# One branch for all left-over work, row numbers at the seam, spread planning, and global keys filled once, in a fused attention and mixture-of-experts kernel

## The chip, the cores and the metric

The kernel runs on one core of a Trainium2 chip. The metric is the time of one execution on the device in microseconds (us), where less is better. A core has a matrix engine (PE, with its weight loads listed as PEld), a vector engine (DVE), a scalar engine (ACT), a general engine (POOL), and SP, which here only issues DMAs. Each takes its own list of instructions in order and waits for the others by semaphores. An indirect DMA (gather or scatter by row numbers) is issued by POOL.

## The reference

An attention over 4 batches, 8 heads, 768 positions and 64 features feeds a mixture of experts with one expert for each token.

```python
scores = q @ k.T / sqrt(64)                       # per batch and head
keep   = (key < 8) | (0 <= query - key < 96)      # 8 global keys, 96 local ones
scores = where(keep, scores - slope[head] * dist, -1e9)
x      = softmax(scores) @ v                      # -> 3072 tokens of 512 features

logits = x @ w_gate + modality_bias[modality_id]  # 8 experts
e      = argmax(logits);  g = softmax(logits)[e]
out    = g * (relu(x @ w1[e]) @ w2[e])            # 512 -> 1024 -> 512
```

## The kernel before

**Attention.** The 3072 queries are 24 blocks of 128, six for each batch (`NB`). `step(n)`, for n from 0 to 24, writes down by hand the order of PE, ACT and DVE. It works on several blocks at once: scores of block n (`s_mm`, L257), maximum and bias (`red`, DVE L276) and exponential (ACT L287) of its eight heads; transposes of the probabilities of block n-1 (`t_mm` L301, `t_cp` L310 on DVE or L308 on ACT); probabilities times V of block n-2 (`pv`, L322 with the local V rows `vl`, L334 with `vo` and `va`), its scaling (`xr`, L355) and its store; the gate logits of older blocks (`gate_a`, `gate_b`, `gate_c`); and the transposes of the next block's keys and queries (`k_mm` L215, `k_cp`: keys by ACT L228, queries by DVE L224). The lists of POOL and SP are made by a scheduler, which also decides where anything stands that the hand-written order leaves open.

**Keys.** The key store `kt` has fourteen slots of 72 columns, two for each block and two ahead of them. A slot begins with the 8 global keys. These come with the batch's first block, and POOL copies them into the other slots: L231 two for each block, L233 one for a batch. The scores read whole slots.

**Routing.** `at(n, f)` adds f to the end of step n. Each batch's tokens are routed in parts (`route_a`, `route_b`, `route_d`), and `route_c` has POOL scatter the token numbers into a sorted list in memory (`ids_sorted`, L450). When two batches are routed, `plan_e` works out on DVE, in four parts, the first three expert slots (e0 to e2). For these, `ld_x` asks for the token lists (`uie`, L618), `gather_x` gathers the tokens (L623), `ld_w` loads weights, and `split` splits these into a high part (ACT, L656) and a low part (DVE, L657). `copyv` is POOL's copy of V rows into `vo` (L135, L137).

**Experts.** `x_t` transposes the gathered tokens (L668) and splits them (ACT L671, DVE L672); `l1_unit` is the first layer (L685 to L687, results L691 and L692), `l2` the second (L723 to L725). `fin` multiplies by the gate and has POOL scatter the result (L738) by row numbers `oi`, made at L730 from the token list. Fourteen slots follow one another in a hand-written order.

**The end.** Tokens that fit into no slot are left to a loop, and other values of `n_global` and `n_local` to a general path. With these inputs neither has work:

```python
    general = nc.values_load(flag[0:1, 0:1], min_val=0, max_val=1)
    with tc.If(general):
        general_path()
    ...
    count = nc.values_load(lcnt[0:1, 0:1], min_val=0, max_val=NLT)
    with tc.For_i(0, count, 1) as g:
```

Of the kernel before, what the change touches and what calls it, by code (L numbers as in the profile page):

```python
# [9 lines left out]
F32 = mybir.dt.float32  # L10
# [9 lines left out]
P = 128  # L20
# [47 lines left out]
def moe_attention_kernel(ctx, tc, q, k, v, n_global, n_local, modality, w_gate, mod_bias, w1, w2, out):  # L68
# [141 lines left out]
    def k_mm(n, which):  # L210

        bank = p_t(f"tr{n}_{which}")
        src = kqn[n][which]
        for hp in range(NP):
            nc.tensor.transpose(  # L215
                bank[:, hp * P : (hp + 1) * P], src[:, 2 * hp : 2 * hp + 2].rearrange("p h d -> p (h d)"), ident
            )
        kqn[n][which] = bank

    def k_cp(n, which):  # L220
        bank, i = kqn[n][which], n % NB
        if which:
            qts[n] = pp.tile([P, NP, P], F32, tag="qt", name=f"qt{n}", bufs=2)
            V.tensor_copy(qts[n].rearrange("p a b -> p (a b)"), bank)  # L224
            return
        slot = kt[:, :, PER * (i + 1) : PER * (i + 2)].rearrange("p a (c w) -> p a c w", w=CH)
        view = bank.rearrange("p (a c w) -> p a c w", a=NP, c=2)
        last[0] = nc.scalar.copy(slot[:, :, :, NG0:], view)  # L228
        first = kt[:, :, PER + NG0 : PER + 2 * NG0]
        for c in range(2):  # L230
            nc.gpsimd.tensor_copy(slot[:, :, c, 0:NG0], first)  # L231
        if i == 0:
            nc.gpsimd.tensor_copy(kt[:, :, CH : CH + NG0], first)  # L233
# [325 lines left out]
    def granules(uex, ust, uli):  # L559
# [38 lines left out]
        V.tensor_copy(lcnt, m)  # L598
        yield
# [30 lines left out]
    def ld_w(s, parts="ab"):  # L630
        if "a" in parts:
            s.e = nc.sync.value_load(s.e_src, min_val=0, max_val=E - 1)
        e = s.e
        for which, src in (("a", w1), ("b", w2)):
            if which not in parts:
                continue
            for c in range(4):
# [89 lines left out]
    def fin(s, ts, parts=1):  # L727
        if 0 in ts:
            s.oi = idp.tile([P, 2], I32, tag="oi", name=f"oi{s.name}")
            V.tensor_tensor(s.oi[:, 0 : s.halves], s.ui[:, 0 : s.halves, 0], s.inv, ALU.add)  # L730
        for t in ts:
            ob = mp.tile([P, DM], F32, tag="ob", name=f"ob{s.name}{t}", bufs=2)
            gate = s.ui.bitcast(F32)[:, t, 1:2]
            n = DM // parts
            nc.scalar.mul(ob[:, 0:n], s.po[t][:, 0:n], gate)  # L735
            if parts == 2:
                V.tensor_scalar(ob[:, n:], s.po[t][:, n:], gate, None, ALU.mult)
# [200 lines left out]
    flag = const.tile([P, 1], I32, name="flag")  # L938
    lte = const.tile([P, NLT], I32, name="lte")
# [128 lines left out]
    for j in range(4):  # L1068
        at(LAST + j // 2, plan_e)
# [12 lines left out]
    at(LAST + 1, lambda: ld_w(eslots[0], "a"))  # L1082
    at(LAST + 3, lambda: [ld_x(s) for s in eslots])
    at(LAST + 4, lambda: [gather_x(s) for s in eslots[:GE]])
    for j in range(4):
        at(LAST + (4, 5, 6, 6)[j], split, None, "a", j)
    at(LAST + 4, lambda: ld_w(eslots[0], "b"))

    def l1_first(f):
        if f == 0:  # L1090
            x_t(eslots[0], 0)
            x_t(eslots[0], 1)
            l1_begin(eslots[0])
        l1_unit(eslots[0], f)
# [22 lines left out]
    def step(n):  # L1117
# [25 lines left out]
        if more:  # L1143
# [105 lines left out]
    for u in range(nslot):  # L1249
# [28 lines left out]
        else:  # L1278
            fin(s, [s.halves - 1], 2)
# [12 lines left out]
    wrawb = None  # L1292
    wraw = ctx.enter_context(tc.tile_pool(name="wraw2", bufs=8))
    wsp = wspb = ctx.enter_context(tc.tile_pool(name="wsp2", bufs=1))
    xgp = ctx.enter_context(tc.tile_pool(name="xgp2", bufs=1))
    idp = ctx.enter_context(tc.tile_pool(name="idp2", bufs=1))
    mp = ctx.enter_context(tc.tile_pool(name="mp2", bufs=1))
    count = nc.values_load(lcnt[0:1, 0:1], min_val=0, max_val=NLT)
    with tc.For_i(0, count, 1) as g:
        iv = idp.tile([P, 1], F32, tag="iv", name="iv")  # L1300
        V.tensor_copy(iv, ltv[:, ds(g, 1)])
        s = mk("l", lte[0:1, ds(g, 1)], lto[0:1, ds(g, 1)], iv, xd, 1)
        s.straight = False
        ld_x(s)
        ld_w(s)
        gather_x(s)
        x_t(s, 0)
        for c in range(4):
            split(s, "a", c)
        l1_begin(s)  # L1310
        for fh in range(2):
            l1_gran(s, fh)
            split(s, "b", 2 * fh)
            split(s, "b", 2 * fh + 1)
            l1_gran_t(s, fh)
        for c in range(8):
            l2(s, c, 0)
        fin(s, [0])
# [38 lines left out]
```

## Time and profile before

| | |
|---|---|
| median of 3 runs | 521.53 us (519.7 to 525.9) |
| the profiled execution | 518.35 us |
| its span in the trace | 516.2 us |
| mean granted PE clock | 0.961 |
| first scores of step 0 / 1 / 2 | 13.34 / 19.35 / 26.75 us |
| a usual step | 6.46 us (step 4 at 40.60, step 5 at 47.06) |
| steps 19 to 22 begin | 141.41, 149.45, 157.21, 172.55 us |
| last output scatter issued | 502.74 us |

The time includes some 2 us around the span. Times inside the trace are counted from the span's start. A row of the timeline gives the start, the duration, the engine, the line, the operation with its output and input, and in brackets the idle time before it and what ended that. A suffix q (SPq, POOLq) is the engine's sequencer: loads of registers, branches, DMA issues.

### The profile page before, as it was taken

Reading aid. Unit: us, or ns where it says so; the run is one execution under the profiler, and the core shown is the slowest. Engines: PE = TensorE matmul, PEld = TensorE weight load, DVE = VectorE, ACT = ScalarE, POOL = GpSimd, SP = SyncE. Lnnn points to the kernel's source line nnn. Section 1 sums busy time; section 2 is a strip of 40 time slices with the busy share of each in tenths; the row PEclk is TensorE's granted clock in tenths of the full one; section 3 lists DMA queues with packets and bytes.
Section 4 is the critical chain, followed back from the end, with each engine's and each line's share of the span. In section 5 each row is a group of like instructions: output and inputs, shape, how many; then the busy total and the mean of one; then the engine's idle time right before and its main releaser. Section 6 shows DMA issues by size and latency. Waiting matters only on the chain.

```text
span 516.2 us, 15203 instructions
## 1 busy us (share of the span) xinstructions
PE 472.8 (92%) x5789; PEld 423.2 (82%) x5789; DVE 340.9 (66%) x992; ACT 297.3 (58%) x716; POOL 162.3 (31%) x282
## 2 busy tenths in 40 slices
PE   4889999999985988999999999899999999999980
PEld 4778899899874867898989898798978998798960
DVE  2488788888893883788874657564765658557410
ACT  3668777777754672555454557554665558545420
POOL 9703414545552354042322215204041031400110
PEclk8599999999999898999999999999999999999995
DMA  9678889778676736367877658778597667953100
GB/s 179 143 211 189 193 190 210 178 169 209 142 203 184 235 125 187 130 247 236 251 236 234 236 197 295 248 248 273 163 332 254 227 228 250 332 187 123 42 23 23
DMA packets 125508, 102.74 MB, mean 199 GB/s; under 512 B 96283, under 2 KB 97715, under 8 KB 125428
## 3 DMA queue, kind: packets, MB, share of 16 engines
q1 hardware_dynamic: 120660, 88.65, 59.6%
q0 software_dynamic: 4768, 13.05, 7.1%
q8 instruction: 47, 0.77, 0.6%
q14 instruction: 33, 0.27, 0.2%
HBM read 87.31 MB, written 14.63 MB: 197 GB/s over the span
## 4 chain that ended last, share of the span: by engine, by line
PE 77%; DVE 7%; ACT 5%; DMA 3%; issue 3%; SPq 2%; POOL 0%; POOLq 0%; ACTq 0%; DVEq 0%
PE s L257 6%; PE phs L687 6%; PE phs L685 6%; PE phs L686 6%; PE pt L301 5%; PE pos L725 5%; PE pos L724 5%; PE pos L723 5%; PE x L334 4%; PE tr L215 3%; ACT pr L287 3%; PE x L322 3%; PE phe L685 2%; PE phe L686 2%; PE phe L687 2%
## 5 line engine op out<-in xcount | busy, mean ns | idle before, releaser
L287 ACT ACTIVATE pr<-sc,nmx 128x168 f32<-128x168 f32 x192 | 81.1, 423 | 42.0 <-DVE nmx L276 42.0
L687 PE MATMUL phs<-xhs,als 128*128 128x256 f32 x256 | 72.5, 283 | 0.5 <-DVE als L657 0.5
L685 PE MATMUL phs<-xhs,ahs 128*128 128x256 f32 x256 | 72.2, 282 | 0.0
L686 PE MATMUL phs<-xls,ahs 128*128 128x256 f32 x256 | 72.1, 282 | 0.0
L623 POOL DMA_INDIRECT xgs<-x_rows,uis x16 | 27.5, 1716 | 130.5 <-DMA uis<-ids_sorted 66.6
L276 DVE CUSTOM_DVE_ANT_0 sc<-s,tbl 128x168 f32<-128x168 f32 x192 | 52.2, 327 | 21.4 <-PE s L257 18.2
L301 PE MATMUL pt<-ident,pr 128*128 128x128 f32 x288 | 47.7, 290 | 9.7 <-DVE pT L310 6.7
L692 DVE SCALAR_TENSOR_TENSOR hls<-phs,hhs 128x512 fp32r<-128x512 f32 x32 | 22.1, 692 | 50.4 <-ACT hhs L691 50.4
L257 PEld LDWEIGHTS s<-kt,qt 64*64 64x64 f32 x1536 | 40.6, 139 | 15.9 <-POOL kt L233 7.7
L257 PE MATMUL s<-kt,qt 64*64 64x128 f32 (+1 forms) x1536 | 44.6, 258 | 9.5 <-POOL kt L233 6.7
L723 PE MATMUL pos<-bhs,hhs 128*128 128x512 f32 x128 | 51.4, 401 | 0.0
L725 PE MATMUL pos<-bhs,hls 128*128 128x512 f32 x128 | 50.6, 395 | 0.0
L724 PE MATMUL pos<-bls,hhs 128*128 128x512 f32 x128 | 50.5, 395 | 0.0
L687 PEld LDWEIGHTS phs<-xhs,als 128*128 128x128 f32 x256 | 48.8, 191 | 0.8 <-DVE als L657 0.7
L685 PEld LDWEIGHTS phs<-xhs,ahs 128*128 128x128 f32 x256 | 48.9, 191 | 0.4
L686 PEld LDWEIGHTS phs<-xls,ahs 128*128 128x128 f32 x256 | 48.8, 191 | 0.4
L691 ACT ACTIVATE hhs<-phs 128x512 fp32r<-128x512 f32 x32 | 19.1, 597 | 49.8 <-PE phs L687 49.8
L310 DVE COPY pT<-pt 128x384 f32<-128x384 f32 x71 | 39.1, 550 | 9.6 <-PE pt L301 9.4
L301 PEld LDWEIGHTS pt<-ident,pr 128*128 128x128 f32 x288 | 32.4, 145 | 15.5 <-DVE pT L310 8.0
L450 POOL DMA_INDIRECT ids_sorted<-tki,pi x24 | 24.6, 1023 | 39.6 <-DVE remb L508 23.6
L287 ACT ACTIVATION_READ_ACCUMULATOR pr<-sc,nmx 128x1 f32 x192 | 35.9, 187 | 0.0
L738 POOL DMA_INDIRECT out<-obs,ois x16 | 17.1, 1069 | 47.6 <-ACT obs L735 39.7
(340 smaller groups left out, 1257.6 us busy)
## 6 DMA issues: line engine op xcount, KB each, us to landing
va<-in_v SPq DMA_DIRECT2D x25, 256.0 KB, 3.5
kn<-in_k SPq DMA_DIRECT2D x24, 256.0 KB, 4.9
qn<-in_q SPq DMA_DIRECT2D x24, 256.0 KB, 4.8
x_rows<-xr SPq DMA_DIRECT2D x24, 256.0 KB
vl<-in_v SPq DMA_DIRECT2D x84, 32.0 KB, 3.3
rawe0a<-in_moe_w SPq DMA_DIRECT2D x4, 512.0 KB, 3.6
rawe0b<-in_moe_w SPq DMA_DIRECT2D x4, 512.0 KB, 3.6
rawe1a<-in_moe_w SPq DMA_DIRECT2D x4, 512.0 KB
```

The lines of the kernel that those rows point to most:

```text
L257: nc.tensor.matmul(ps[h][64 * half : 64 * half + 64, c : c + cnt], qt[hs, hp, 64 * half : 64 * half + 64], keys, start=True, stop=True,)
L276: V.tensor_tensor_reduce(out=sc, in0=pss[n, hp // 2][h][:, hp % 2 * W : (hp % 2 + 1) * W], in1=(tbl0 if n % NB == 0 else tbl)[:, hh, :], o ...
L287: last[0] = nc.scalar.activation(pr[:, h * (PRW - W) : h * (PRW - W) + W], sc, AF.Exp, bias=nmx[:, hh : hh + 1], scale=-1.0, accum_out=sum ...
L301: nc.tensor.transpose(tp[:, j * P : (j + 1) * P], pr[:, o : o + P], ident)
L310: V.tensor_copy(pT.rearrange("p a b -> p (a b)"), tp[:, 0 : 3 * P])
L623: nc.gpsimd.indirect_dma_start(out=s.xg[:, t, :], out_offset=None, in_=s.xsrc, in_offset=bass.IndirectOffsetOnAxis(ap=s.ui[:, t, 0:1], axi ...
L685: nc.tensor.matmul(o, hi[:, fs], s.xh[:, c, :], start=(c == 0), stop=False)
L686: nc.tensor.matmul(o, hi[:, fs], s.xl[:, c, :], start=False, stop=False)
L687: nc.tensor.matmul(o, lo[:, fs], s.xh[:, c, :], start=False, stop=(c == 3))
L723: nc.tensor.matmul(s.po[t], s.hh[:, fc, tt], hi[:, wv], start=(fc == 0), stop=False)
L724: nc.tensor.matmul(s.po[t], s.hh[:, fc, tt], lo[:, wv], start=False, stop=False)
L725: nc.tensor.matmul(s.po[t], s.hl[:, fc, tt], hi[:, wv], start=False, stop=(fc == 7))
```

## The change

1. **One branch.** A flag `past`, which is the larger of "tokens left over" and the general path's flag, is worked out with the plan. A single `If` on it encloses the general path and the left-over loop.
2. **Row numbers.** `rows_out` makes `oi` for e0 to e2 after the last gate instead of where the scheduler had put it.
3. **Plan.** The four parts of `plan_e` stand in steps 17, 18, 18, 19 (18, 18, 19, 19 before).
4. **Splits.** The four weight splits of e0 stand in steps 21, 22, 23, 24 (22, 23, 24, 24 before), and its first weights are loaded in two pieces, in steps 19 and 20.
5. **Global keys.** With a batch's first block all slots are filled at once: DVE fills slots 1 to 3, POOL slots 4 to 13.
6. **Queries and keys of block 1** (positions 128 to 255) are transposed in step 0 behind its scores, and copied behind four of its heads.
7. **Seam.** The token transposes of e0 stand ahead of block 23's `pv`, its first layer behind that, and the last gates are reordered.
8. **Last output.** Both halves on ACT (before, one on ACT and one on DVE).
9. Constants are loaded and made a step later, the zeroing of the list (`consts_c`) one piece for each step.

```diff
-        bank = p_t(f"tr{n}_{which}")
+        bank = (p_p if n == 1 else p_t)(f"tr{n}_{which}")
...
-        first = kt[:, :, PER + NG0 : PER + 2 * NG0]
-        for c in range(2):
-            nc.gpsimd.tensor_copy(slot[:, :, c, 0:NG0], first)
         if i == 0:
-            nc.gpsimd.tensor_copy(kt[:, :, CH : CH + NG0], first)
+            first = kt[:, :, PER + NG0 : PER + 2 * NG0].unsqueeze(2)
+            for eng, c0, c1 in ((V, 1, 4), (nc.gpsimd, 4, 2 * NB + 2)):
+                eng.tensor_copy(slots[:, :, c0:c1, 0:NG0], first.broadcast_to([P, NP, c1 - c0, NG0]))
...
+        V.tensor_scalar(m, m, 1.0, None, ALU.min)
+        V.tensor_copy(m2, flag)
+        V.tensor_tensor(m, m, m2, ALU.max)
+        V.tensor_copy(past, m)
...
+    def rows_out(s):
+        s.oi = idp.tile([P, 2], I32, tag="oi", name=f"oi{s.name}")
+        V.tensor_tensor(s.oi[:, 0 : s.halves], s.ui[:, 0 : s.halves, 0], s.inv, ALU.add)
...
-            n = DM // parts
-            nc.scalar.mul(ob[:, 0:n], s.po[t][:, 0:n], gate)
-            if parts == 2:
-                V.tensor_scalar(ob[:, n:], s.po[t][:, n:], gate, None, ALU.mult)
+            nc.scalar.mul(ob, s.po[t], gate)
...
-    at(0, consts_l)
-    at(2, consts_b)
+    at(1, consts_l)
+    at(3, consts_b)
     for j in range(8):
-        at(3 + j // 2, consts_c, j)
-    at(3, consts_d)
+        at(3 + j, consts_c, j)
+    at(4, consts_d)
...
-        at(LAST + j // 2, plan_e)
+        at(LAST - 1 + (0, 1, 1, 2)[j], plan_e)
...
-    at(LAST + 1, lambda: ld_w(eslots[0], "a"))
+    at(LAST + 1, lambda: ld_w(eslots[0], "a", (0, 1)))
+    at(LAST + 2, lambda: ld_w(eslots[0], "a", (2, 3)))
...
-        at(LAST + (4, 5, 6, 6)[j], split, None, "a", j)
+        at(LAST + (3, 4, 5, 6)[j], split, None, "a", j)
...
             s_mm(n, 1)
+            if not n:
+                k_mm(1, 0)
+                k_mm(1, 1)
             for hh in (0, 2, 1, 3, 4, 6, 5):
                 red(n, hh)
+                if not n and hh == 3:
+                    k_cp(1, 0)
+                    k_cp(1, 1)
...
-    l1_first(0)
+    x_t(eslots[0], 0)
+    x_t(eslots[0], 1)
+    l1_begin(eslots[0])
     rinv(NBLK - 1)
     pv(NBLK - 1)
+    gate_a(*gates(NBLK - 2))
     gate_c(*gates(NBLK - 3))
     xr(NBLK - 1)
-    gate_a(*gates(NBLK - 2))
-    l1_first(1)
+    l1_first(0)
...
+    for s in eslots:
+        rows_out(s)
     l1_first(3)
...
-    general = nc.values_load(flag[0:1, 0:1], min_val=0, max_val=1)
-    with tc.If(general):
-        general_path()
+    any_left = nc.values_load(past[0:1, 0:1], min_val=0, max_val=1)
+    with tc.If(any_left):
+        leftover()      # For_i(0, general): general_path(); then the left-over loop
```

Three places of the engines' lists show what moved. The first is POOL's list from the first key copies on, before the change (`tbl` are pieces of the bias tables, `kt` the key store):

```order
L231 COPY kt<-kt 128x4x8 x2
L205 TENSOR_SCALAR tbl<-mm 128x168
L205 TENSOR_SCALAR tbl<-mm 128x40
L205 TENSOR_SCALAR tbl<-mm 128x128
...
L205 TENSOR_SCALAR tbl<-mm 128x128
L233 COPY kt<-kt 128x4x8
L231 COPY kt<-kt 128x4x8 x4
L135 COPY vo_80<-va_76 64x512
```

And DVE's list at the same place after it (`mm` feeds the tables, `qt` are transposed queries, `sc` the scores of a head):

```order
L193 TENSOR_TENSOR mm<-mm,dd 128x168
L194 TENSOR_TENSOR mm_181<-mm_181,dd 128x168
L233 COPY kt<-kt 128x4x3x8
L224 COPY qt_260<-tr_1_255 128x512
L276 ISA sc_0_331,nmx_330<-s_0_0_283,tbl_169 128x168
```

The copy of L233, which stood behind twelve table pieces on POOL, now stands for slots 1 to 3 on DVE between L194 and the query copy; POOL's own part (128x4x10x8) stands ahead of the twelve pieces.

The second place is DVE's list in step 21, before the change (`oie` are row numbers, `uie` the token lists, `pT` transposed probabilities):

```order
L345 TENSOR_SCALAR rin_3987<-sums_3568 128x8
L346 RECIPROCAL rin_3987<-rin_3987 128x8
L730 TENSOR_TENSOR oie_5016<-uie_4105,inve 128x2
L730 TENSOR_TENSOR oie_5375<-uie_4116,inve 128x2
L730 TENSOR_TENSOR oie_5647<-uie_4127,inve 128x2
L310 COPY pT_0_4028<-pt_0_4024 128x384
L276 ISA sc_7_4036,nmx_3965<-s_1_1_3947,tbl 128x168
```

After it they stand behind the attention's last gate logits (`lgt`):

```order
L388 TENSOR_TENSOR lgt_4255<-lq_4_4665,tbias 128x8
L388 TENSOR_TENSOR lgt_4255<-lq_5_4681,tbias 128x8
L735 TENSOR_TENSOR oie_4684<-uie_4064,inve 128x2
L735 TENSOR_TENSOR oie_4686<-uie_4075,inve 128x2
L735 TENSOR_TENSOR oie_4688<-uie_4086,inve 128x2
L399 TENSOR_REDUCE mx_4821<-lgt_4255 128x6
```

So nothing on DVE in step 21 reads the token lists any more.

The third place is PE's list (weight loads left out) at the seam, before the change (`mte` are transposed tokens of e0, `phe` its first layer, `x` the attention's output):

```order
L668 MATMUL mte_4593<-ident,xge_4314 128x128 x4
L668 MATMUL mte_4600<-ident,xge_4314 128x128 x4
L685 MATMUL phe_4609<-xhe_4591,ahe_4320 128x256
L686 MATMUL phe_4609<-xle_4592,ahe_4320 128x256
L687 MATMUL phe_4609<-xhe_4591,ale_4321 128x256
...
L322 MATMUL x_0_4625<-vl_86,pT_0_4538 64x64 x2
```

And after it:

```order
L673 MATMUL mte_4550<-ident,xge_4275 128x128 x4
L673 MATMUL mte_4557<-ident,xge_4275 128x128 x4
L322 MATMUL x_0_4569<-vl_86,pT_0_4499 64x64 x2
...
L334 MATMUL x_1_4570<-va_79,pT_3_4528 64x64
L369 MATMUL tx_4_4603<-ident,xr_4507 128x128 x4
L387 MATMUL lq_3_4610<-sel,lps_3_4546 128x8
L690 MATMUL phe_4617<-xhe_4548,ahe_4088 128x256
L691 MATMUL phe_4617<-xle_4549,ahe_4088 128x256
```

The first layer, which followed the token transposes directly, now follows all of block 23's probabilities times V (L322, L334) and a part of the gates.

More of the change, by code (lines that the diff above doesn't have):

```diff
@@ L225, in k_cp @@
             return
-        slot = kt[:, :, PER * (i + 1) : PER * (i + 2)].rearrange("p a (c w) -> p a c w", w=CH)
+        slots = kt.rearrange("p a (c w) -> p a c w", w=CH)
         view = bank.rearrange("p (a c w) -> p a c w", a=NP, c=2)
-        last[0] = nc.scalar.copy(slot[:, :, :, NG0:], view)
-        first = kt[:, :, PER + NG0 : PER + 2 * NG0]
-        for c in range(2):
-            nc.gpsimd.tensor_copy(slot[:, :, c, 0:NG0], first)
+        last[0] = nc.scalar.copy(slots[:, :, 2 * i + 2 : 2 * i + 4, NG0:], view)
         if i == 0:
-            nc.gpsimd.tensor_copy(kt[:, :, CH : CH + NG0], first)
+            first = kt[:, :, PER + NG0 : PER + 2 * NG0].unsqueeze(2)
+            for eng, c0, c1 in ((V, 1, 4), (nc.gpsimd, 4, 2 * NB + 2)):
+                eng.tensor_copy(slots[:, :, c0:c1, 0:NG0], first.broadcast_to([P, NP, c1 - c0, NG0]))
     blk, pss, pts, gt, lgts, rt, xrs = {}, {}, {}, {}, {}, {}, {}
@@ L628, in gather_x, with ld_w @@
             )
-    def ld_w(s, parts="ab"):
-        if "a" in parts:
+    def ld_w(s, parts="ab", cs=range(4)):
+        if "a" in parts and 0 in cs:
             s.e = nc.sync.value_load(s.e_src, min_val=0, max_val=E - 1)
@@ L636, in ld_w @@
                 continue
-            for c in range(4):
+            for c in cs:
                 pool = wrawb if wrawb is not None and nraw[0] % (RA + RB) >= RA else wraw
@@ L1142, in step @@
             t_cp(n - 1, 2)
-        if more:
+        if more and n:
             k_mm(n + 1, 1)
@@ L1284, in moe_attention_kernel @@
     sM.close()
-    general = nc.values_load(flag[0:1, 0:1], min_val=0, max_val=1)
-    with tc.If(general):
-        general_path()
[L1292 to L1318, printed above, removed]
+    def leftover():
+        nonlocal wrawb, wraw, wsp, wspb, xgp, idp, mp
+        general = nc.values_load(flag[0:1, 0:1], min_val=0, max_val=1)
+        with tc.For_i(0, general, 1):
+            general_path()
+        with ExitStack() as g:
+            wrawb = None
+            wraw = g.enter_context(tc.tile_pool(name="wraw2", bufs=8))
+            wsp = wspb = g.enter_context(tc.tile_pool(name="wsp2", bufs=1))
+            xgp = g.enter_context(tc.tile_pool(name="xgp2", bufs=1))
+            idp = g.enter_context(tc.tile_pool(name="idp2", bufs=1))
+            mp = g.enter_context(tc.tile_pool(name="mp2", bufs=1))
+            count = nc.values_load(lcnt[0:1, 0:1], min_val=0, max_val=NLT)
+            with tc.For_i(0, count, 1) as j:
+                iv = idp.tile([P, 1], F32, tag="iv", name="iv")
+                V.tensor_copy(iv, ltv[:, ds(j, 1)])
+                s = mk("l", lte[0:1, ds(j, 1)], lto[0:1, ds(j, 1)], iv, xd, 1)
+                s.straight = False
+                ld_x(s)
+                ld_w(s)
+                gather_x(s)
+                x_t(s, 0)
+                for c in range(4):
+                    split(s, "a", c)
+                l1_begin(s)
+                for fh in range(2):
+                    l1_gran(s, fh)
+                    split(s, "b", 2 * fh)
+                    split(s, "b", 2 * fh + 1)
+                    l1_gran_t(s, fh)
+                for c in range(8):
+                    l2(s, c, 0)
+                fin(s, [0])
```

21 lines of the change are left out of this document (9 added, 12 removed).

## The prediction

> **What bounds the kernel now.** I read the page first, for the engine that is busy almost all the time and for the clock it was granted, and then the waits of that engine, to see where it stands still.
>
> ```profile
> span 516.2 us, 15203 instructions
> PE 472.8 (92%) x5789; PEld 423.2 (82%) x5789; DVE 340.9 (66%) x992; ACT 297.3 (58%) x716; POOL 162.3 (31%) x282
> ```
>
> PE is busy for 472.8 of 516.2 us, so at most 43 us stand idle, plus whatever PE loses by running at a lower clock. The profiled execution took 518.35 us, 2.15 us more than its span. Next the waits of PE (us in total, times, longest):
>
> ```profile
> PE s L257 <- POOL kt L233: 6.7, 4, 5.8
> PE pt L301 <- DVE pT L310: 6.7, 4, 4.2
> PE htg L711 <- DVE hlg L715: 3.1, 3, 1.0
> PE pt L301 <- issue: 2.5, 1, 2.5
> PE phe L685 <- ACT xhe L671: 2.1, 1, 2.1
> PE phe L686 <- DVE xle L672: 1.1, 1, 1.1
> ```
>
> The longest sits at the scores' wait for the global keys (L233), the next at the copy of transposed probabilities (L310), two at the first layer of the first expert slot (L685, L686). Only the `htg` waits lie inside the expert phase, which the diff does not touch before its last output. So the change can win only at the start, in the attention steps, at the seam to the expert phase and behind the last matmul, and I cost it place by place.
>
> **A. The start.** The timeline's first 27 us (start, duration, engine, line; at the end the idle time before and what ended it):
>
> ```profile
> 5.90 0.58 ACT L228 COPY kt<-tr 128x512 f32<-128x512 f32 x1 [3.83 <-PE tr L215]
> 6.34 0.69 DVE L224 COPY qt<-tr 128x512 f32<-128x512 f32 x1
> 6.55 0.35 POOL L231 COPY kt<-kt 128x32 f32<-128x32 f32 x2
> 6.99 6.03 POOL L205 TENSOR_SCALAR tbl<-mm 128x168 f32<-128x168 f32 x12
> 7.30 2.34 ACT L203 ACTIVATE tbl<-mm 128x168 f32<-128x168 f32 x12 [0.82 <-DVE mm L194]
> 13.34 2.84 PE L257 MATMUL s<-kt,qt 64*64 64x40 f32 x62 [5.77 <-POOL kt L233]
> 19.35 2.86 PE L257 MATMUL s<-kt,qt 64*64 64x128 f32 x64 [1.27 <-ACT kt L228]
> 26.75 1.51 PE L257 MATMUL s<-kt,qt 64*64 64x128 f32 x56 [0.35 <-ACT kt L228]
> ```
>
> POOL makes twelve pieces of the bias tables (6.03 us) ahead of the one small copy at L233, and step 0's scores stand behind it until 13.34. After the change DVE fills slots 1 to 3 directly behind the key copy, which ends at 6.48. By POOL's 0.18 us for 32 elements and DVE's own 0.69 us for 512, 96 elements take 0.2 to 0.35 us. The query copy then follows on DVE (it was ahead), 0.69 us, and the scores run at about 7.5 instead of 13.34: **5.8 us**.
>
> The keys of block 1 are now transposed right behind those scores, and their ACT copy stands behind four exponentials of step 0 instead of eight. Two rows of the page price them:
>
> ```profile
> L287 ACT ACTIVATE pr<-sc,nmx 128x168 f32<-128x168 f32 x192 | 81.1, 423 | 42.0 <-DVE nmx L276 42.0
> L287 ACT ACTIVATION_READ_ACCUMULATOR pr<-sc,nmx 128x1 f32 x192 | 35.9, 187 | 0.0
> ```
>
> Four times 0.42 + 0.19 is 2.4 us; I take **2.2**, since the scores of all eight heads come first anyhow. Step 1's scores then begin near 11.35 instead of 19.35, 8.0 us earlier. From step 1 to step 2 the old run took 7.40 us. A usual step is the distance between these two:
>
> ```profile
> 40.60 1.55 PE L257 MATMUL s<-kt,qt 64*64 64x128 f32 x62
> 47.06 1.17 PE L257 MATMUL s<-kt,qt 64*64 64x128 f32 x40
> ```
>
> That is 6.46. The stretches of 2 us (duration, busy time of PE, PEld, DVE, ACT, POOL, then granted clock, DMA time, GB/s) say why the early steps are slower:
>
> ```profile
> 10.00:12.00 2.00, 0.00 (x0) 0.00 (x0) 0.00 (x0) 0.00 (x0) 1.94 (x4) 0.50 1.28 208
> 26.00:28.00 2.00, 1.65 (x60) 1.41 (x62) 1.52 (x8) 0.58 (x1) 0.00 (x0) 1.00 0.90 313
> ```
>
> PE stood idle for 5.77 us ahead of 13.34, and the clock is 0.50 there; it is 1.00 again at 26. If the gap shrinks to under 1 us the half clock should not come, and 0.94 us more are to be had. I take 0.7 of them, because another thing is late next: POOL's tables for four heads still end near 13.0, and step 0's last heads and all of step 1's exponentials queue behind them on ACT. **A = -8.7.** The Trainium skill's page TensorE: Matmul & The Clock Gate (Part 1: The HAM clock gate) says that PE falls to half clock after an idle window of about 3.4 us and rises again after as long a busy one. The rows above agree with its fall. By it alone, with no gap of that length left, A would be some 1.2 us more, -9.9; I keep that as the far end of A.
>
> The near end: 12 pieces ending at 13.0, eight exponentials behind them (4.9 us) and the next key copy give step 2 at about 19, which is -7.7; and if the earlier steps only run into loads that have not landed (1.28 of every 2 us of the DMA engines are busy at 10 to 12), half of it, -4, is left.
>
> One rule speaks against the fill. The Trainium skill's page SBUF — State Buffer (SBUF: two separate sides) says that VectorE and GpSimd share a port pair that the one which starts first holds for its whole instruction. As a mechanism here: POOL's fill of slots 4 to 13 is released by the same key copy as DVE's, and if POOL goes first, DVE waits for it, 0.18 us at least (one slot at L231's price) and 1.75 at most (ten slots). The sum would be that much less. No row of this trace shows such a block; 1 in 3.
>
> **B. Batches 1 to 3.** At step 6 the scores stood behind the same small copies:
>
> ```profile
> 54.52 1.39 PE L257 MATMUL s<-kt,qt 64*64 64x40 f32 x53 [0.57 <-POOL kt L233]
> ```
>
> The slots are filled once now, so this wait goes at steps 6 and 12: 2 x 0.57 = **-1.2**. At step 18 I count nothing, as a plan piece is put there. Ends: 0 and -2.
>
> **C. Plan pieces a step earlier.** They are the same DVE instructions at other places. Steps 19 and 20 are long now, as the rows in D show (8.04 and 7.76 us against 6.46), so spreading them could help, but step 17 carries a routing part already. I take **0**, ends -0.8 and +0.8 (half of the surplus of a long step).
>
> **D. Row numbers out of step 21.** Steps 19 to 22 and POOL beside them:
>
> ```profile
> 141.41 0.82 PE L257 MATMUL s<-kt,qt 64*64 64x128 f32 x24
> 149.45 1.55 PE L257 MATMUL s<-kt,qt 64*64 64x128 f32 x62
> 157.21 1.55 PE L257 MATMUL s<-kt,qt 64*64 64x128 f32 x62
> 159.21 0.96 POOL L450 DMA_INDIRECT ids_sorted<-tki,pi  x1 [0.30 <-issue]
> 164.41 2.18 SPq L618 DMA_DIRECT2D uie<-ids_sorted  x3
> 166.69 0.16 DVE L730 TENSOR_TENSOR oie<-uie,inve 128x2 int32<-128x2 int32 x1 [6.24 <-DMA uie<-ids_sorted]
> 167.62 1.01 POOL L623 DMA_INDIRECT xge<-x_rows,uie  x1 [7.44 <-DVE oie L730]
> 171.44 0.94 POOL L623 DMA_INDIRECT xge<-x_rows,uie  x1 [0.30 <-issue]
> 172.55 1.72 PE L257 MATMUL s<-kt,qt 64*64 64x128 f32 x58
> 180.73 1.16 POOL L137 COPY vo<-va 64x512 f32<-64x512 f32 x1 [7.70 <-DMA xge<-x_rows,uie]
> 187.03 0.27 PE L334 MATMUL x<-vo,pT 128*64 128x64 f32 x1
> ```
>
> DVE stands 6.24 us at three tiny additions that wait for the list of rows; behind them in its queue are L310's copies, and PE waits for those (4.2 of the 6.7 us above). Step 21 takes 15.34 us, step 20 takes 7.76; the difference, 7.6 us, goes with the additions, and PE would reach L334 of block 22 at 179.4. (A 2.5 us stop of PE at "issue" lies inside the same step; DVE was standing at the list during it, so it cannot be added.)
>
> But another chain runs beside it and does not get shorter: the last scatter is issued by 160.2, the list is asked for at 164.4, lands at 166.6, four gathers are issued up to 172.4, the last one lands at 180.7, and only then does POOL, in its order, copy the V rows (L137, 1.16 us) that block 22's L334 multiplies. The old gathers began 0.9 us after the list; without DVE beside them I give 0.8 of that back, and the copy ends near 181.1 instead of 181.9. PE therefore meets a **new wait of some 1.7 us** at L334, and D is 187.0 - 181.1 = **-6.0**. Ends: -2, if the gathers are issued or land later among the transfers that are now closer together; -8.5, if the chain shrinks with the steps.
>
> **E. Seam to the expert phase.** Today the transposes of the first slot are followed at once by its matmuls: the waits of 2.1 and 1.1 us above, and the clock drops:
>
> ```profile
> 193.00:198.00 5.00, 3.09 (x44) 2.67 (x44) 2.52 (x5) 0.73 (x2) 3.78 (x5) 0.84 0.66 215
> ```
>
> After the change the probabilities times V of block 23 stand in that gap. They last over 2 us, and one weight split fewer stands on DVE ahead of L672. So 3.2 us of waits go, and with them the lower clock, 0.16 of 5 us, 0.8: **-4.0**, ends -1.2 (the DVE part alone) and -5.2.
>
> **F. The tail.** Behind the last matmul:
>
> ```profile
> 501.47 0.47 ACT L735 ACTIVATE obs<-pos,uis 128x256 f32<-128x256 f32 x1 [4.89 <-PE pos L725]
> 501.98 0.48 DVE L737 TENSOR_SCALAR obs<-pos,uis 128x256 f32<-128x256 f32 x1 [8.93 <-ACT obs L735]
> L1298 SPq TENSOR_LOAD <-lcnt x1: 278/278/278, 505.5 to 505.5; - x1
> L1299 POOLq COMPARE_BRANCH  x3: 33/38/45, 506.0 to 509.0; - x3
> L1353 POOLq DRAIN  x3: 40/103/6125, 509.2 to 515.9; - x3
> ```
>
> The second flag load and the empty loop take from 505.5 to 509.0; one branch decides both now, so 3.6 us go. The last output half took 0.47 and 0.48 us one after the other; a whole one costs about 0.65 on ACT, -0.3. **F = -3.9**, ends -4.5 and -0.3, the latter if POOL's 6.1 us drain waits for something that ends at a fixed time after the last output. DVE's four extra operations of a plan part cost under 1 us where DVE has time: nothing.
>
> Left at nothing: the constants moved a step later (DVE and POOL have room in steps 3 to 10), weight loads in two pieces (the same bytes), the expert phase itself (PE-bound; a shift of its loads by up to 1.5 us either way is within its 3.1 us of waits).
>
> **Sum.** -8.7 - 1.2 + 0 - 6.0 - 4.0 - 3.9 = -23.8, so 494.5 for the profiled execution. The median of the runs shown, 521.53, stands 0.6% above that execution; in proportion **497.5 us**.
>
> **Rivals.** (1) The start wins half: loads or tables hold step 2, A = -4, 502. For: DMA is busy 64% of the time then. Against: no wait of PE on a DMA among the rows of waits. 0.12. (2) The stall comes back at L334, D = -2: 501.5. For: the chain of list and gathers is all latency. Against: it was as long before. 0.15. (3) The drain keeps the end where it is, F = -0.3: 501. For: its 6.1 us are the longest thing in the tail. Against: it begins only after the loop. 0.12. (4) The change does not do what it says, DVE's fill runs behind POOL's: 0.2 to 1.75 us as worked out in A, so 498 to 499; at 1 in 3 it lies inside each other case and moves none out of its bounds. (5) Slower: the altered order at the seam leaves PE at half clock into the expert phase, where it has no idle time to hide it. 62 score matmuls took 2.84 us at 0.50 (row 13.34) and 1.55 at full clock (row 40.60), 1.83 times as long. So the gain of 24 us is gone when 29 us of that phase's work run so, for 53 us; at 70 us it is 531. Against: the old run falls to 0.50 only after a long stop and recovers by 26. 0.03. (6) More than forecast, the far ends of A and D together: 492, 0.08. My forecast's own case, 494 to 500, has 0.5.
>
> The range of 8 in 10 takes in cases 1 to 3, two of them at once, and most of 6: 490 to 506. About 1% is what a measurement of this kernel can tell from no change; faster by more than that means under 516.3, which all cases but (5) and a pile-up of (1), (2), (3) give: 0.94, within 1% 0.04, slower 0.02.
>
> **What will show it.** A: scores of step 0 near 7.5 and of step 2 near 18, clock near 1.00 from 8 to 26. B: no wait of L257 on POOL. D: step 21 under 8 us and a short wait at L334 for POOL's V copy; that wait at 5 us would be rival 2. E: no wait at the first expert matmuls (L690, L691 after). F: one flag load behind the last output and a drain that starts 3.6 us sooner after it. What would make it wrong is a wait that I have not priced: PE on a DMA in steps 1 to 6, or a lower clock after the seam.

## The result, and the profile after

| | before | after |
|---|---|---|
| median | 521.77 us (4 runs) | 505.89 us (4 runs, 503.07 to 508.88) |
| ratio after / before | | 0.9687, 95% interval 0.9598 to 0.9776 |
| the profiled execution, its span | 518.35, 516.2 us | 504.03, 502.2 us |
| mean granted PE clock | 0.961 | 0.987 |

The change makes the kernel faster by 3.1%, some 16 us, where 24 were forecast. Ratios, here and below, leave out executions that took over 1.5% longer than the fastest of the same kernel. The page after it, first line and engines, and then the waits of PE (us in total, times, longest):

```profile
span 502.2 us, 15068 instructions
PE 468.6 (93%) x5789; PEld 419.4 (84%) x5789; DVE 343.1 (68%) x999; ACT 297.5 (59%) x716; POOL 156.3 (31%) x234
```

```profile
PE pt L301 <- DVE pT L310: 4.7, 6, 1.6
PE htg L716 <- DVE hlg L720: 3.1, 3, 1.0
PE x L322 <- DMA vl<-in_v: 1.9, 2, 1.1
PE s L257 <- ACT kt L228: 1.8, 3, 1.1
PE pt L301 <- issue: 1.7, 1, 1.7
PE s L257 <- DVE qt L224: 1.6, 1, 1.6
PE x L334 <- issue: 1.4, 1, 1.4
PE tx L369 <- DVE nmx L276: 1.1, 1, 1.1
```

The four waits that the change aimed at are gone: the keys from POOL, the 4.2 us at L310 in step 21, and both of the first layer. New ones stand in the list, and for the one on V rows (`vl`) the prediction had no term in its sum. The table below takes both traces apart at points that both pass: how far the changed kernel is ahead there, what it won or lost since the point above, and what the prediction had for that stretch.

| point | before | after | ahead | since the point above | forecast |
|---|---|---|---|---|---|
| scores of step 2 | 26.75 | 17.41 | 9.3 | -9.3 | A: -8.7 |
| step 4 | 40.60 | 35.15 | 5.5 | +3.9 | 0 |
| step 8 | 67.43 | 63.87 | 3.6 | +1.9 | B: -0.6 |
| step 18 | 134.34 | 130.66 | 3.7 | -0.1 | B: -0.6 |
| step 20 | 149.45 | 148.78 | 0.7 | +3.0 | C: 0 |
| L334 of block 22 | 187.03 | 179.66 | 7.4 | -6.7 | D: -6.0 |
| first matmul of slot s0 | 272.01 | 261.53 | 10.5 | -3.1 | E: -4.0 |
| last matmul ends | 501.39 | 491.12 | 10.3 | +0.2 | 0 |
| end of the span | 516.15 | 502.23 | 13.9 | -3.7 | F: -3.9 |

A, D, E and F came as forecast, within 0.9 us each. What is missing was lost again in three stretches that the sum had at nothing or at a small gain: steps 2 to 4, steps 4 to 8, and steps 18 to 20.

**Start and step 3.** The timeline of the changed kernel (start, duration, engine, line, and the idle time before):

```profile
6.41 0.53 POOL L233 COPY kt<-kt 128x320 f32<-128x320 f32 x1
6.55 0.45 DVE L233 COPY kt<-kt 128x96 f32<-128x96 f32 x1
7.75 1.59 PE L257 MATMUL s<-kt,qt 64*64 64x128 f32 x64 [1.64 <-DVE qt L224]
...
17.41 1.55 PE L257 MATMUL s<-kt,qt 64*64 64x128 f32 x62 [0.35 <-ACT kt L228]
...
22.02 2.15 SPq L122 DMA_DIRECT2D vl<-in_v  x4
23.81 1.61 PE L257 MATMUL s<-kt,qt 64*64 64x128 f32 x64 [0.35 <-ACT kt L228]
26.16 0.30 PE L322 MATMUL x<-vl,pT 40*64 40x64 f32 x2 [0.75 <-DMA vl<-in_v]
27.57 0.85 PE L322 MATMUL x<-vl,pT 40*64 40x64 f32 x30 [1.11 <-DMA vl<-in_v]
35.15 1.10 PE L257 MATMUL s<-kt,qt 64*64 64x128 f32 x37
```

Steps 0 to 2 begin at 7.75, 11.46 and 17.41, as worked out (7.5, 11.35, 18). Then step 3 takes 11.3 us. Its `pv` multiplies block 1's V rows, which the program loads twice, ahead of the steps and again in step 0 (so in the kernel before, too). SP issues the second load only at 22.02, behind two more query and key loads and the constants, and PE stops for it twice, 1.9 us. A further 0.8 us is a transposition of modality numbers, which stood in step 2 before. Most of the rest follows from the clock:

```profile
25.28:28.69 3.41, 1.55 (x51) 1.25 (x45) 2.12 (x14) 2.98 (x14) 1.46 (x3) 1.00 0.57 121
28.69:32.10 3.41, 3.41 (x39) 3.29 (x35) 1.17 (x5) 0.48 (x2) 0.98 (x2) 0.50 0.58 172
```

In the first of these stretches PE is busy for 1.55 of 3.41 us (the number behind the duration), and in the next the granted clock (before the last two) is 0.50, although no single stop was longer than 1.11 us.

**Steps 18 to 20.** The first row is from the kernel before, the others, DVE and POOL at the end of step 17's list, from the changed kernel:

```profile
143.01 0.17 DVE L492 TENSOR_SCALAR first_used<-cexe 128x8 f32<-128x8 f32 x1
...
133.36 1.28 POOL L142 COPY vl<-vg 8x512 f32<-8x512 f32 x2 [2.18 <-PE x L322]
133.44 0.55 DVE L492 TENSOR_SCALAR first_used<-cexe 128x8 f32<-128x8 f32 x1
134.03 0.64 DVE L493 TENSOR_SCALAR first_used<-first_used 128x8 f32<-128x8 f32 x1
134.69 0.60 POOL L135 COPY vo<-va 64x512 f32<-64x512 f32 x1
134.70 0.62 DVE L494 TENSOR_TENSOR first_used<-first_used,fulle 128x8 f32<-128x8 f32 x1
135.24 0.32 DVE L276 CUSTOM_DVE_ANT_0 sc<-s,tbl 128x168 f32<-128x168 f32 x1
...
134.50:137.91 3.41, 1.02 (x9) 0.57 (x7) 3.34 (x20) 2.31 (x11) 1.34 (x3) 1.00 0.73 160
```

Three operations on 8 columns take 0.55 to 0.64 us where the kernel before has 0.17 for each, and each ends within 0.04 us of a copy of POOL (at 134.00, 134.64 and 135.29). Behind them stand step 18's maxima (L276): scores ready at 132.3 are first taken at 135.24, PE runs dry (busy 1.02 of 3.41 us in the last row, a stretch like those above), the clock falls to 0.50 at 137.9, and step 18 takes 10.98 us.

**Row numbers.** A stop of PE in step 21, POOL's V copy after the gathers, block 22's L334, and what follows:

```profile
160.64 0.55 PE L301 MATMUL pt<-ident,pr 128*128 128x128 f32 x3 [1.74 <-issue]
...
176.65 0.61 POOL L137 COPY vo<-va 64x512 f32<-64x512 f32 x1 [5.88 <-DMA xge<-x_rows,uie]
179.66 0.27 PE L334 MATMUL x<-vo,pT 128*64 128x64 f32 x1
180.95 0.28 POOL L433 TENSOR_TENSOR pos<-pos,oh 128x48 f32<-128x48 f32 x1
181.26 0.20 DVE L442 TENSOR_REDUCE pf<-pos 128x6 f32<-128x48 f32 x1 [1.71 <-POOL pos L433]
183.68 0.88 PE L301 MATMUL pt<-ident,pr 128*128 128x128 f32 x6 [1.63 <-DVE pT L310]
```

Step 21 goes from 15.3 to 8.3 us. In the kernel before, PE's stop at "issue" lay inside the time that DVE stood at the row numbers; that wait is gone, the stop is still there, and it now costs 1.7 us of its own. The V copy is done 2.4 us ahead of L334, so PE does not wait there. But POOL's list was held until 176.65 by the same gathers, and behind the copies in it stands the routing of the last batch (up to L433). DVE waits 1.7 us for that, and PE 1.6 us for DVE: the wait that D had foreseen, in size and cause, at another place, and 4 us later.

**Tail.**

```profile
492.44 0.98 POOL L744 DMA_INDIRECT out<-obs,ois  x1 [4.87 <-ACT obs L743]
L1374 POOLq DRAIN  x3: 40/107/6122, 495.3 to 502.0; - x3
```

POOL's last drain is as long as before (6.1 us), but the first of the drains begins 2.9 us behind the last scatter's issue instead of 6.5: F.

### The profile page after: what moved, and what is told of

Read it like the earlier page. It is cut to its first block, busy times and chain, and to the rows that moved or that the text cites. A ratio compares the mean times of both kernels' runs of the same rounds, so it can differ in the third digit from the quotient of the medians.

```text
span 502.2 us, 15068 instructions
## 1 busy us (share of the span) xinstructions
PE 468.6 (93%) x5789; PEld 419.4 (84%) x5789; DVE 343.1 (68%) x999; ACT 297.5 (59%) x716; POOL 156.3 (31%) x234
## 4 chain that ended last, share of the span: by engine, by line
PE 44%; issue 12%; DVE 2%; DMA 2%; POOL 1%; ACT 0%; SPq 0%; POOLq 0%; DVEq 0%; ACTq 0%
PE phs L692 5%; PE phs L690 4%; PE phs L691 4%; PE pos L730 4%; PE pos L729 4%; PE pos L728 4%; PE phe L690 2%; PE phe L691 2%; PE phe L692 2%; PE poe L728 2%; PE poe L730 2%; PE poe L729 2%; DMA uig<-ids_sorted 2%; POOL out L744 1%; PE mts L673 1%
## 5 line engine op out<-in xcount | busy, mean ns | idle before, releaser
L690 PE MATMUL phs<-xhs,ahs 128*128 128x256 f32 x256 | 72.2, 282 | 0.0
L691 PE MATMUL phs<-xls,ahs 128*128 128x256 f32 x256 | 72.1, 282 | 0.0
L276 DVE CUSTOM_DVE_ANT_0 sc<-s,tbl 128x168 f32<-128x168 f32 x192 | 52.1, 327 | 9.4 <-PE s L257 9.4
L301 PE MATMUL pt<-ident,pr 128*128 128x128 f32 x288 | 47.2, 288 | 7.3 <-DVE pT L310 4.7
L310 DVE COPY pT<-pt 128x384 f32<-128x384 f32 x71 | 38.9, 548 | 15.5 <-PE pt L301 15.4
L690 PEld LDWEIGHTS phs<-xhs,ahs 128*128 128x128 f32 x256 | 48.9, 191 | 0.4
L691 PEld LDWEIGHTS phs<-xls,ahs 128*128 128x128 f32 x256 | 48.8, 191 | 0.3
L257 PEld LDWEIGHTS s<-kt,qt 64*64 64x64 f32 x1536 | 38.2, 132 | 10.4 <-ACT kt L228 6.1
L257 PE MATMUL s<-kt,qt 64*64 64x128 f32 (+1 forms) x1536 | 41.7, 248 | 4.7 <-ACT kt L228 1.8
L301 PEld LDWEIGHTS pt<-ident,pr 128*128 128x128 f32 x288 | 32.4, 144 | 13.1 <-DVE pT L310 5.4
```

The source lines that it names most:

```text
L257: nc.tensor.matmul(ps[h][64 * half : 64 * half + 64, c : c + cnt], qt[hs, hp, 64 * half : 64 * half + 64], keys, start=True, stop=True,)
L276: V.tensor_tensor_reduce(out=sc, in0=pss[n, hp // 2][h][:, hp % 2 * W : (hp % 2 + 1) * W], in1=(tbl0 if n % NB == 0 else tbl)[:, hh, :], o ...
L301: nc.tensor.transpose(tp[:, j * P : (j + 1) * P], pr[:, o : o + P], ident)
L310: V.tensor_copy(pT.rearrange("p a b -> p (a b)"), tp[:, 0 : 3 * P])
L690: nc.tensor.matmul(o, hi[:, fs], s.xh[:, c, :], start=(c == 0), stop=False)
L691: nc.tensor.matmul(o, hi[:, fs], s.xl[:, c, :], start=False, stop=False)
```

## The experiments

Kernels sent together ran on one chip, beside the kernel before. The chips differ: the kernel before took 540.7 us with the first four, 541.9 with the next four and 522.8 with the last four. So ratios are compared inside a set, and steps by their traces.

**V rows once.** In step 0's load:

```diff
-        if n + LV < NBLK:
+        if n and n + LV < NBLK:
```

> The changed kernel, with block 1's V rows loaded once (before the steps) and not a second time in step 0. Theory V: the second load stands on SP behind the constants, is issued at 21.5 to 23.7 and lands at 26 to 27.5; PE stops 1.9 us for it in step 3 and falls to half clock. Without it no wait of PE on vl in step 3, that step 11.3 -> 7.0 to 7.8 us (0.8 for the transposition of the modality numbers stays), span 502.2 -> 498 to 499. Rival: step 3 is long because of the modality numbers moved into it and a general backlog of loads; then step 3 stays at 10 or more and the span within 1 us of 502.

No wait of PE on `vl` was left. Step 3 begins and ends at these rows:

```profile
24.37 1.55 PE L257 MATMUL s<-kt,qt 64*64 64x128 f32 x62 [0.35 <-ACT kt L228]
31.99 1.22 PE L257 MATMUL s<-kt,qt 64*64 64x128 f32 x46
```

That is 7.6 us, inside theory V's 7.0 to 7.8, and the rival's 10 is excluded; the granted clock stayed at 1.00 there. The next step then waited 0.9 us for keys. The time, 0.9895 of before (0.9855 to 0.9935), says nothing about the gain, since the changed kernel itself did not run on this chip. The expected span could not be read either: 530.5 us.

**Plan parts back.**

```diff
-        at(LAST - 1 + (0, 1, 1, 2)[j], plan_e)
+        at(LAST + j // 2, plan_e)
```

> The changed kernel, with the four plan parts back in steps 18, 18, 19, 19. Theory P: the part in step 17 stands ahead of step 18's maxima on DVE, and its last three operations run beside POOL's copies and last 0.55 to 0.64 us instead of 0.17; that starves ACT and PE, and half clock follows. Then those three take 0.17 us again where no POOL copy runs, step 18 10.98 -> 7.1, steps 19 and 20 rise to about 8.0 and 7.7, steps 18 to 20 together 24.6 -> 22.9, span about 500.5. Rival: step 18 is long because of the key fill and the scatters; then it stays above 9.5 and the span at 502 or more.

```profile
138.22 1.62 PE L257 MATMUL s<-kt,qt 64*64 64x128 f32 x55
144.90 1.32 PE L257 MATMUL s<-kt,qt 64*64 64x128 f32 x49
146.44 0.17 DVE L492 TENSOR_SCALAR first_used<-cexe 128x8 f32<-128x8 f32 x1
...
146.85 0.17 DVE L494 TENSOR_TENSOR first_used<-first_used,fulle 128x8 f32<-128x8 f32 x1
```

Step 18 took 6.68 us and the three operations 0.17 each, as theory P had it. Steps 19 and 20 could not be read for it: 10.4 us each on this chip. The time was 0.9801 of before (0.9744 to 0.9859), the span 524.8 us.

**Both.**

> Both of these edits in one kernel. By V and P together the span is 496 to 497 and the median 498.5 to 500.5, against 505.9 for the changed kernel; if the two gains are the same slack spent twice (what waits next is the list of rows and the gathers, a chain of its own from step 20 on), the span is 498 or more.

Time 0.9835 of before (0.9784 to 0.9886); the span of 532.4 us does not tell the two cases apart, since both were worked out for the other chip. Inconclusive here, so it was run again (last set).

**Row numbers alone**, `rows_out` in the kernel before, called behind its last gate.

> The kernel before, with only the row numbers of e0 to e2 moved behind the attention's last gate. By the prediction's step D, step 21 goes from 15.3 to under 8.4 us, the stretch from step 20 to block 22's L334 from 37.6 to 31 us, and the span from 516.2 to 509 to 510. Rival: the wait returns at L334 behind POOL's V copy; then L334 waits 4 us or more and the span is 513 or more.

It missed: 1.0022 of before (0.9992 to 1.0052). No wait at L334 came, so the rival is not the reason. The two rows are steps 20 and 21 (duration; busy time of PE, PEld, DVE, ACT, POOL; clock; DMA):

```profile
163.31:173.69 10.38, 9.35 (x167) 8.43 (x163) 7.34 (x39) 5.26 (x20) 3.15 (x4) 0.84 0.90 272
173.69:184.60 10.91, 9.37 (x167) 8.49 (x163) 5.10 (x25) 5.38 (x20) 4.83 (x5) 0.84 0.43 104
```

Step 21 takes 10.9 us with no DVE stall in it, and step 20 as much: on this chip PE stopped at "issue" for 0.3 to 0.5 us twice in each of them, and the clock averaged 0.84. What the stall costs on such a chip can be read from the kernel with one branch alone (below), which has the additions at their old place: DVE stands at them for 3.07 us at first, not 6.24, step 21 takes 12.0 us, and from step 20 to block 22's L334 it takes 38.9 us against 37.4 without them. So the stall was worth some 1.5 us there, which is less than these times can show (the two kernels ran on different chips of this kind). On a chip like that of the first result the edit was not run alone.

**The changed kernel again.**

> The changed kernel once more, so that it stands beside the runs of one chip. The runs of the last four kernels stood on a chip where the kernel before took 540.7 us instead of 521.8, with stretches (steps 13 to 15 and 19 to 22) in which PE's own instructions came late. Theory: where that happens the gain shrinks, because steps 19 to 22 are then bound by PE's instructions and the stall at the row numbers costs little; ratio to before 0.975 to 0.985 there. Without such stretches the ratio is 0.965 to 0.975 again.

Ratio 0.9805 (0.9744 to 0.9867), inside the range given for chips with such stretches.

**Start alone**: key fill and block 1's transposes in the kernel before, constants left where they were.

> The kernel before, with only the key fill and block 1's transposes in step 0; the constants are loaded where they were. By the prediction's step A, step 2 starts 9 us earlier (26.75 -> 17.5) and all of it stays, span 8 to 10 us shorter. Theory V: the second load of block 1's V rows is now wanted 9 us earlier, but without the constants between it comes at about 19 to 21 instead of 21.5 to 23.7, so step 3 takes 7 to 9 us and 6 to 8 us of the gain stay. Rival: the early steps are bound by loads altogether, step 3 takes 11 us as in the changed kernel, 4 to 5 us stay.

Step 2 began at 17.23, and step 3 took 9.8 us, with a wait of 1.1 us for `vl` still there. The load that PE waits for was issued at 24.51, later than in the changed kernel, and the constants still stand ahead of it on SP (13.98 to 16.6). So moving the constants back does not bring the load in time, and whether they or the query and key loads make it late is not shown. Step 3's length lies between the two theories (7 to 9, and 11). Beside the next kernel, which ran in the same set with the old start, step 4 was 3.8 us ahead (35.06 against 38.88) and step 8 5.0 us, the rival's 4 to 5. The time, 0.9839 of before (0.978 to 0.9898), is 8.7 us less, but that leaves out seven of the twelve runs; the median of all twelve, 537.36 us, is 4.6 us less than before, close to what the start kept. In the trace the kernel gets further ahead in steps 13 to 15, which took 20.9 us against 30.4 in the next kernel, where PE stopped at "issue" nine times and the clock fell three times; no part of the edit touches these steps.

**One branch alone** in the kernel before.

> The kernel before, with only the one branch around the general path and the left-over loop (the last output still in two halves). By the prediction's step F, from the last output scatter's issue to the end of the span 13.4 -> 9.8 us, 3.6 us less, and 0.993 of the time. Rival: the drain ends at a fixed time after the last output, then 13 us or more.

From the last scatter's issue (527.09) the first drain begins 3.5 us later, and the span ends 10.6 us later (13.4 in the profile of the kernel before):

```profile
L1364 POOLq DRAIN  x3: 40/107/6261, 530.6 to 537.4; - x3
527.09 0.98 POOL L743 DMA_INDIRECT out<-obs,ois  x1 [4.90 <-DVE obs L742]
```

That is 2.9 us less by the trace, 0.7 short of what was expected, and 0.9908 of the time (0.9869 to 0.9947). The drain does not end at a fixed time after the last output, so the rival falls.

**Old seam** in the changed kernel.

> The changed kernel, with the old order at the seam (token transposes, first layer, then block 23's probabilities times V) and the row numbers still behind the last gate. By the prediction's step E, the first matmuls of e0 wait 2 to 3 us again, and from block 22's L334 to the first matmul of slot s0 it takes 3 to 4 us more than in the changed kernel on the same chip. Rival: the new order only moves the wait; then less than 1 us more.

Ratio 0.9733 (0.9641 to 0.9824), overlapping with the changed kernel's 0.9805, and from two of its six runs; the medians of all six, 534.95 and 531.81 us, point the other way: inconclusive. In its trace the first matmuls of e0 wait 2.0 us again (1.1 for ACT, 0.9 for DVE), but from block 22's L334 to slot s0 it takes 94.6 us against 94.0 in the changed kernel's trace of this set, 0.6 more, as the rival had it; but both are single traces of executions that the ratios leave out, so this settles nothing. On these chips the new order met a wait of its own. In the trace of the kernel with the plan parts back, DVE stands still for 6.8 us at the seam for something that the trace does not name, with xr(23), for which PE waits, queued behind it:

```profile
208.19 0.17 DVE L388 TENSOR_TENSOR lgt<-lq,tbias 128x8 f32<-128x8 f32 x1 [6.84 <-remote]
```

In the changed kernel's first trace the same operation stands at 188.71 without a wait. All four traces of the new order on these two chips have the wait, 6.8 to 8.4 us, and the trace of the old order has none, so it takes back E's gain there. What DVE waits for stays open.

**Third set**, on a chip like the first result's: the changed kernel, both edits, and two single runs.

> The changed kernel, as the reference of this set of runs. Theory: ratio to before 0.965 to 0.985, the lower the fewer stops of PE for its own instructions there are in steps 12 to 22.

> Block 1's V rows loaded once and the plan parts back in steps 18, 18, 19, 19, beside the changed kernel on one chip. Theory: the two losses that the traces showed (3.7 us in step 3, 1.7 in steps 18 to 20) are recovered where PE is not stopped for its instructions, 3 to 6 us less than the changed kernel. Rival: a wait behind (the list of rows, or PE's instructions) takes them back, less than 2 us.

The changed kernel: 508.12 us, 0.9717 of before (0.9668 to 0.9767). With both edits: **503.45 us, 0.9622 (0.9575 to 0.9669)**, 4.7 us less, inside the 3 to 6 expected; the intervals just touch. It is the lowest median of the kernels tried. Its trace had no wait on `vl`, but a stop of another kind in step 3 (29.80 below), so that step still took 10.6 us there (11.1 in the changed kernel of this set). Steps 18 to 20 took 8.79, 8.06 and 7.81 us, 1.9 of it a stop at issue; the remaining 22.8 us are what theory P had (22.9). But the changed kernel took only 23.4 us for them in this set, since its step 18 met no half clock. So the two traces, 505.0 and 507.1 us long, do not show where 4.7 us come from.

**Fewer warming matmuls.** `WARM = 20` instead of 40 (one run, 510.31 us).

> The changed kernel with 20 warming matmuls instead of 40 at its start; nothing else moves. The stops of PE at issue stood at the same matmul in every kernel, counted from the start (the 1111th in step 7, about the 2358th in step 15). Theory: they belong to places in PE's list of instructions as it lies in memory; then they stay at those counts and so fall 20 matmuls later in the code. Rival: they belong to what runs beside them in the code; then they stand 20 counts earlier, at the 1091st and 2338th.

Stops of PE at issue, one fence for each trace: the changed kernel (the first trace and that of this set), both edits, V copies on ACT (next), and WARM = 20:

```profile
59.90 0.27 PE L334 MATMUL x<-vo,pT 128*64 128x64 f32 x1 [1.39 <-issue]
```

```profile
110.18 0.22 PE L334 MATMUL x<-vo,pT 128*64 128x64 f32 x1 [2.26 <-issue]
```

```profile
29.80 0.22 PE L334 MATMUL x<-va,pT 128*64 128x64 f32 x1 [2.94 <-issue]
```

```profile
62.62 0.37 PE L335 MATMUL x<-vo,pT 128*64 128x64 f32 x1 [2.76 <-issue]
113.67 0.22 PE L335 MATMUL x<-vo,pT 128*64 128x64 f32 x1 [1.53 <-issue]
```

```profile
63.01 0.44 PE L301 MATMUL pt<-ident,pr 128*128 128x128 f32 x2 [0.43 <-issue]
110.93 0.66 PE L215 MATMUL tr<-ident,qn 128*128 128x128 f32 x4 [0.32 <-issue]
117.46 0.22 PE L334 MATMUL x<-va,pT 128*64 128x64 f32 x1 [2.11 <-issue]
```

Counted from the start of the program (from 0), 59.90, 62.62 and 63.01 are the 1111th matmul, 110.18, 113.67 and 110.93 the 2256th, 29.80 the 474th and 117.46 the 2383rd. With WARM = 20 the counts stayed and the code moved by 20: at 1111 and 2256 the stops are no longer in L334 (one line later in the kernel with the copies on ACT) but in L301 and L215. That is the theory; the rival's 1091 did not occur. Neither 2338 nor the 2358th that was named occurred: that one was a stop of 0.4 us in six traces of the slower chips. All stops over 0.8 us on this kind of chip stand at the 474th, 1111th, 2256th, 2383rd, 2892nd or 3402nd (or one beside it), which are multiples of 127.3 apart. A matmul comes with a weight load, so that is 255 instructions, and the page has the packets of instructions:

```profile
q8 instruction: 47, 0.77, 0.6%
```

0.77 MB in 47 packets is 16.4 KB for each, 64 bytes for each of 255 instructions; PE's 5789 matmuls with their weight loads would fill 45.5 such packets. So these stops seem to stand where one packet of PE's own list ends and the next begins; that this queue brings PE's list is inferred from its size. The stop of 2.5 us at L301 that the prediction's rows show as "issue" is the 3402nd. Which of the places stops, and for how long, changes from run to run. On the slower chips there are more stops, most of 0.3 to 0.6 us and at other counts, for which this gives no account; and what makes a packet late was not settled.

**V copies of blocks 17 and 20 on ACT**, so that no copy of POOL stands beside the plan part in step 17.

> The changed kernel with the V copies of blocks 17 and 20 on ACT instead of POOL, so that the plan part at the end of step 17 has no copy of POOL beside it. Theory: L492 to L494 (here one line later) take 0.17 us each again instead of 0.55 to 0.64, and step 18 goes from 10.98 to 9.7 us or less, part of it because the clock does not fall. Rival: their length comes from something else, they stay over 0.4 us and step 18 near 11.

```profile
140.41 0.17 DVE L493 TENSOR_SCALAR first_used<-cexe 128x8 f32<-128x8 f32 x1
...
140.83 0.17 DVE L495 TENSOR_TENSOR first_used<-first_used,fulle 128x8 f32<-128x8 f32 x1
```

The three take 0.17 us, and step 18 8.49 us. The changed kernel of this set is the one to compare with: the three took 0.55, 0.64 and 0.62 us there too, and step 18 took 9.77 us with no half clock. So, by one trace each, POOL's copies beside them cost 1.3 us, and the half clock of the first trace's 10.98 a further 1.2. With both edits, where the parts stand in steps 18 and 19, step 18 took 6.9 us without its stop at issue; the 1.6 us from there to 8.49 go with the place ahead of the maxima. As a version it is no gain (512.69 us, one run).

## Why the prediction was right or wrong

The sign was right, and the time lay inside the range, but only just (505.89 in 490 to 506; two of the four runs lay above it). That it did not fall outside is luck: the forecast itself, 497.5, was 8.4 us too low, and on the profile the sum was 9.5 us too good (494.5 against 504.03), for reasons that the rivals name at best in part.

- **A, right in its own stretch, wrong in what follows.** -9.3 against -8.7. The step that failed is that the sum takes A in full: it was worked out to step 2, and the lead there was counted as kept, with nothing for the steps behind it. The near end of A ("loads that have not landed", -4) had the right kind of cause at another place: the V rows' second load, 1.9 us, and mostly the half clock that followed, 3.9 us in all. Seven of the eight traces with the early start and the second load have this wait (1.1 to 2.3 us), and the three without that load have none. In the eighth (`WARM = 20`), where step 2 began only at 19.45, step 4 stopped 2.3 us for queries instead, so loads set the pace there too. Rival (1) named step 2, and it is step 3; with -5.5 kept, it is close to the case that had 0.12. Its price of the loads was misread: the 1.28 in the row of 10 to 12 is a share of the DMA engines' time, not us of 2, so they were full there and not busy 64%.
- **B, mis-sized.** -1.2 forecast, from step 6's 0.57 taken twice; step 12's wait in the kernel before was only 0.19. At step 12 it won 0.3 and at step 6 it lost 0.3: DVE's fill at step 6 took 0.51 us instead of 0.21, beside POOL's L142, and the weight loads of the scores wait 0.4 us for it as they had for POOL. Of the 1.9 us lost from step 4 to step 8, 1.4 are the stop at 59.90, which is no effect of the edit: in the third set's trace of the same kernel step 7 has none.
- **The port, as a rival.** By the rows here the three DVE operations, with tiles in SBUF alone, lasted until the copy of POOL beside them ended (0.17 against 0.55 to 0.64 us; back to 0.17 without the copy). That agrees with the Trainium skill, SBUF — State Buffer (SBUF: two separate sides), by which the engine that starts first holds the shared ports for its whole instruction. At the start, where I had weighed it, the fill took 0.45 us instead of the 0.21 that it takes with no copy beside it: 0.24 more, near the low end of 0.2 to 1.75. Its real price fell where I had not looked, in C.
- **C, wrong.** 0 forecast with ends of 0.8; 3.0 lost. The step that failed is "the same DVE instructions at other places": in step 17 they stand ahead of step 18's maxima, beside POOL's copies. By the third set the copies cost 1.3 us, the place 1.6, and the half clock that came in the first trace 1.2.
- **The clock.** I expected no half clock once the long gap was gone. It came twice more, at 28.7 and 137.9, after 3.41 us in which PE was busy 1.55 and 1.02 us, with no stop over 1.3 us in them. The Trainium skill's page TensorE: Matmul & The Clock Gate (Part 1: The HAM clock gate) gives half clock after at least one idle window of about 3.4 us; here windows that PE filled by less than half were enough. That is no threshold: in the same trace the clock stayed at 1.00 after a window with 1.67 us busy (158.42 to 161.83), and on the slower chips it fell after windows with 2.2 to 2.6. Nor did the rows at 13.34 agree with the fall as I said: in the kernel before, the clock fell at 8.62, 1.1 us into that gap, after 3.41 us in which PE was busy 1.49.
- **D, right, with the new wait at another place.** -6.7 against -6.0. The stall went. Step 21 took 8.3 us, where under 8 was named: the stop at "issue" that I left out as hidden in the stall is 1.7 of it. The gathers held POOL as foreseen, but what waited for it was not L334: it was the last batch's routing on DVE, and PE behind that, 1.6 us, which the table counts under E.
- **E, right.** -3.1 against -4.0 on this chip; on the slower ones the wait that the trace does not name takes it back. No wait is left at L690 and L691, the first layer's matmuls; from the token transposes on (190.59 before, 184.97 after) it is -4.9, and the 1.6 us above come off. Alone it could not be measured where it paid.
- **F, right.** -3.7 against -3.9, and -2.9 alone for the branch, for which 3.6 was forecast.

## What to carry to other kernels

When a change brings the start of a pipeline forward, work out for each load of the next steps when it is issued and when it is now wanted, not only whether it bound before: a load that came in good time before becomes the next wait, and one stop of 1 or 2 us can cost a further 2 by the clock. Small operations that are moved are not free by their own duration; look at what stands behind them in the queue, and which copies of POOL run beside them. And when gains are added up, compare the traces at points along the way: here four of six terms were right, and the missing 10 us were lost in stretches that the sum had at nothing or at a small gain.

## What the runs showed of the hardware

- On the faster chips PE stopped at "issue" at fixed counts, multiples of 127.3 matmuls with their weight loads apart (one packet of 16.4 KB), for 0.3 to 3.1 us, not in every run.
- Three DVE operations on 128x8 took 0.17 us each alone and 0.55 to 0.64 us beside copies of POOL.
- The granted clock fell to 0.50 after 3.41 us in which PE was busy 1.55 and 1.02 us, with no stop over 1.3 us.
- The kernel before took 521.8, 540.7, 541.9 and 522.8 us in the four sets, the last three on different chips. In most traces of the slower ones, steps 13 to 15 and 19 to 22 took between 8 and 13.5 us, many of them 10.1 to 10.4, where the changed kernel's first trace has 6.5 to 8.3; in those of 10.3 us the clock was at 0.5 for a third of the step:

```profile
155.25:165.61 10.36, 9.29 (x166) 8.34 (x162) 7.20 (x39) 5.27 (x20) 3.15 (x4) 0.84 0.95 293
```

(Plan parts back, step 20.) There the change was worth 2.0% instead of 3%.
